# A new order table, loads cut differently and less in flight, in a fused attention and feed-forward kernel

## The chip, the cores and the metric

The kernel runs on one NeuronCore of a Trainium2 chip. The metric is the device time of one execution in microseconds (us). Three runs of the kernel before gave 119.25, 120.09 and 119.3 us, median 119.3. The profile is of one further execution, which took 120.38 us; its span on the core, from the first to the last instruction of the program, is 118.6 us, so 1.78 us lie outside the span.

## The reference

The inputs are q, k and v (4 batches, 4 heads, 1088 tokens, 32 features a head), two sketch matrices S1 and S2 (8 x 32), and two feed-forward weights w_in (128 x 2048) and w_out (2048 x 128), all float32.

```
phi(x) = outer(S1 x, S2 x)                 # 64 features per token
kv  = phi(k)^T v ;  z = sum over tokens of phi(k)
x   = phi(q) kv / (phi(q) . z + 1e-6)      # per batch and head, then 4352 x 128
h   = x @ w_in ;  out = (h - tanh(h)) @ w_out
```

So there are two parts: a linear attention whose softmax is replaced by squared sketches, and a feed-forward part with 16 hidden blocks of 128 for 4352 tokens. The term `h @ w_out` is taken as x @ (w_in @ w_out), computed once; that product is kept as a high and a low bfloat16 half (wch and wcl).

## The kernel before, in words

**Names of the work.** An operation has a name and a batch number b from 0 to 3. The k side of a batch is, in this order: kT (VectorE 32x32 transposes of the loaded k, L518), ksk (TensorE sketch, L538), kab (VectorE transposes of the sketch out of PSUM, L544), gram, gm, scmm, sc (a scale from the Gram matrix of the sketches, on TensorE and ScalarE, L559 to L571), three outer products w (VectorE or GpSimd, L579), three kvmm (TensorE, 12 float32 matmuls each, L594), and kvd, kvt, kvb (copies and a transpose of the sum). The q side is qT (VectorE transpose, L530), qsk (TensorE, L633), abc (VectorE transpose out of PSUM, L638), m, den, rd, ap (the division), qp (outer product, L676), qpT (VectorE transpose, L681), num (TensorE, L692), and x, the copies of the result from PSUM into the bfloat16 tile xT (L336). Batch 0 is cut into three pieces of 2, 3 and 4 blocks (num0.0, num0.2, num0.5), batch 1 into two (num1.0, num1.5); batches 2 and 3 are whole. All of this is float32.

**The feed-forward part** goes over ten groups of tokens, of 256, 384, 448, six times 512, and 192. The first three are exactly batch 0, so group 3 (the first of 512) needs the first piece of batch 1. For each group there are 16 matmuls h (L792), 16 tanh on ScalarE (th, L796; the last three groups take two blocks in one instruction), 18 accumulating matmuls o (16 with tanh, L807, and the two with wch and wcl, L811), one transpose ot (VectorE, L816), and stores (L826). The weights are cast to bfloat16 on ScalarE or GpSimd (L336, names wi0 to wi3 and wo0 to wo3); w_in is also transposed on TensorE (wit, L757) and copied (wiT), for the product w_in @ w_out (wc, L771).

**Order.** Nothing is decided while the kernel runs. A text table of some 830 tokens (TABLE) names each operation, the engine that does it, and the buffer that it takes. `plan` (L172) reads the table once; each engine does its share strictly in the table's order, and `sync` adds the semaphore waits. So an instruction that waits holds up all that is behind it on its engine, DMA issues on SyncE and ScalarE included. A token `f` stands for a filler: a matmul of a zero tile (zz, set by a VectorE memset, L398) into an unused bank (L399), which does no work and is there to keep TensorE busy.

**Loads.** All inputs are loaded once (8.8 MB). `load` (L426) adds a limit: before a load is issued, the one that lies CAP bytes of loads before it must have landed. CAP is 2.0 MB. All loads but the two of S1 and S2 are issued by SyncE.

```
load_k:  one DMA of 544 KB a batch (128 partitions)
load_v:  two DMAs a batch, 288 KB and 256 KB, 64 partitions each
load_q:  one of 544 KB a batch; batch 0 in two, 128 and 416 KB
load_wi, load_wo:  four of 256 KB each
```

Of the kernel before, what the change touches and what calls it, by code (L numbers as in the profile page):

```python
# [9 lines left out]
NC = 34  # L10
# [9 lines left out]
CAP = 2.0e6  # L20
# [5 lines left out]
42g 19s 18a 9g 15v 1g 20s 17a 44g 48g 21s 6g 46g 10g 8g 24s 7g 2g 23s 5v 27s 51v:0 52v 40v 28s 41v f f f f f f f f f f  # L26
f f f f f f f f f f f f f 54t:0 0v 13v 22s 16v 53v 26s 4v 50g 25s 56v:0 43g 55v 3g f f f f f 57t:0 62v:0 32s 58a:0
211a f f f 59t 31s 61v:1 60a f f f 70t:0 215a 219t:0 212a 81v f 220t 29s 71v:0 f f 86t:0 221a 63v:2 30s 72v:1 214a
87v:1 f f f f f f f 223t:0 213a 64t:0 73v:0 88v:0 65t 74v:0 89v:1 66t 75v:0 36s 90v:1 76v:0 67a:0 33s f f f f f 68t
91v:1 222t 77v:0 69a:0 f f 78t:0 224a 92v:1 34s 216g 104v:1 79a 80a f f f f f 237t:0 218g 93v:1 233t:1 235t:2 238a:0  # L30
47g 236a:1 f f f 231t:0 105v 217a 245t:2 94t:0 82s 232a:2 97v:2 246a:3 234a:4 255t:0 99v:0 239t:2 95a 247t:1 106t:0
96a 143v:0 248a:5 37s 256a:6 263t:0 38s 144v 240a:7 257t:1 241t:0 310t:2 35s 258a:8 145t:1 107v:1 242a:9 108v 311a:10
39s 225t:0 100v:0 113g:3 259t:1 226t 253t:2 98v 227t 264t 254a:11 265t 266t 146v:0 260a:12 251t:2 267t 286t:1 147v
228t 101t:0 115v:4 229a 287a:13 84s 153g:5 252a:14 230v 249t:1 14v 243t:0 177v:1 306t:2 103a 268t 250a:15 109t:2 85s
244a:16 148t:3 178v 288t:0 102a 83s 269t 149a:1 261t:1 110a:0 270t 307a:17 11g 114v:1 271t 272t 273t 262a:18 179t:0
289a:19 45g 12g 152v:0 274t 275t 357t:0 276t 316t:1 154g:2 277t 181v:1 298t:2 150t 180v 116t:1 299a:2 122v 117t 151a
358a:4 118t 317a:1 155t:0 49g 156t 119a:1 186v:3 157t 182t:3 111t 290t:0 187v:1 158a:0 300t:1 183a:1 120t 112a 159t
188v:4 189t:2 121a:1 160a:2 190t 301a:0 161v 191t 291a:7 184t 349t:1 192a:1 312t:0 278t 185a 193t 350a:9 195v 292t:2
279t 294t:1 194a:3 280t 123t:0 295a:16 281v:0 293a:3 371t:1 313a:5 341t:2 124v:0 318t:0 372a:15 319t 320t 296t:0
342a:14 353t:1 297a:11 365t:2 162t:0 125v:1 354a:6 366a:8 126v:0 302t:0 321t 314t:1 127v:0 303a:12 343t:2 322t 128v:0  # L40
304t:0 344a:18 323t 163v:1 305a:13 359t:2 324t 315a:19 325t 326t 308t:0 360a:7 345t:1 131v:1 327t 309a:3 361t:2 328t
129v:0 346a:16 367t:0 329t 330t 368a:11 331t 355t:1 132v:1 332t 362a:2 369t:0 333t 130v 356a:0 334t 335t 363t:2
370a:12 347t:1 133t:0 164v:0 364a:13 336v:1 348a:17 165v:1 373t:0 138v:2 374t 134a 351t:0 135a 375t 166v:1 376t 352a:3
139v:0 398t:1 400t:2 377t 399a:10 136v:1 378t 406t:0 401a:5 379t 167v:1 402t:1 380t 407a:19 137v 381t 382t 403a:1
424t:2 168v:0 416t:0 383t 425a:14 384t 385t 172v:2 412t:1 417a:18 408t:2 386t 414t:0 409a:16 170v:1 140t:0 413a:17
173v:1 415a:9 387t 396t:1 141a 388t 142a 171v 426t:0 397a:3 389t 390t 473t:2 427a:6 455t:1 391v:2 196t:0 474a:0 169v
395s 456a:4 461t:0 337s 453t:2 428t:0 197v:0 462a:7 339s 429t 418t:1 454a:2 392s 430t 420t:0 404t:2 394s 174t:0
421a:13 198v:1 340s 405a:8 199v:0 393s 419a:11 200v:0 338s 410t:0 201v:0 285s 463t:1 175a 176v 431t 432t 411a:12 433t
206v:2 422t:2 464a:15 434t 510t:0 435t 423a:3 204v:1 436t 457t:1 511a:10 437t 481t:2 202v:0 458a:5 451t:0 438t 482a:1
439t 512t:1 207v:0 440t 452a:8 514t:2 441t 513a:19 205v 442t 443t 515a:16 469t:0 475t:1 203v 444t 470a:12 445t 477t:2  # L50
476a:17 459t:0 446v:2 208t:0 478a:9 450s 460a:18 284s 506t:0 449s 210v 467t:1 508t:2 448s 507a:11 483t:0 209v 484t
468a:13 447s 471t:0 485t 509a:3 486t 465t:1 487t 472a:14 524t:2 488t 466a:6 621t:0 579t:0 525a:8 489t 526t:1 623t:1
580a:2 479t:2 620t 527a:4 490t 516t:0 480a:5 491t 624t 517a:18 492t 493t 532t:1 622a:3 494t 495t 496t 497t 625a:6
518t:0 498t 639t:0 499t 533a:15 500t 536t:2 519a:14 638t 501v:1 534t:1 627t:1 537a:0 522t:0 538t:0 535a:17 539t 520t:2
523a:9 567t:1 540t 521a:5 541t 542t 528t:0 568a:1 543t 544t 529a:11 575t:1 545t 640a:9 626t 546t 547t 530t:0 576a:3
548t 549t 577t:2 531a:10 550t 565t:1 578a:16 551t 552t 628a:4 630t:0 583t:0 553t 554t 584a:14 555t 573t:2 641t:1
566a:5 556v:2 571t:0 629t 574a:4 569t:1 559s 642t 503s 572a:11 597t:0 598t 564s 644t:1 570a:10 645t 581t:0 283s 631a:0
585t:1 505s 646t 599t 600t 502s 586a:15 675t:0 647t 643a:3 282s 601t 648t 504s 602t 603t 604t 582a:17 587t:1 674t
589t:0 588a:5 649t 605t 590a:10 606t 607t 676a:6 595t:1 591t:0 672t:1 608t 671t 592a:11 650t 651t 596a:4 633t:0 609t
673a:1 593t:0 610t 652t 611t 594a:16 632t 635t:1 612t 634a:4 613t 614t 636t 687t:2 615v:0 653t 637a:0 678t:0 654t 616s  # L60
677t 655t 686t 617s 679a:7 721t:1 722t 695t:0 656t 561s 657t 723a:5 658t 619s 681t:0 688a:8 680t 696t 683t:1 659t
682a:2 660t 684t 661t 690t:2 697t 685a:4 662v:1 698t 693t:0 699t 666s 689t 667s 700t 701t 691a:0 618s 702t 703t 724t:1
557s 704t 670s 725t 692t 669s 705t 719t:2 718t 694a:1 706t 664s 707t 560s 562s 708t 709t 720a:9 710t 563s 711t 726a:3
712t 558s 663s 727t:0 728t 734t:1 665s 730t:2 713v:0 731t 668s 742t:1 729a:6 733t 743t 732a:7 736t:0 714s 744t 745t
737t 735a:2 746t 747t 740t:2 739t 715s 748t 738a:4 749t 750t 751t 752t 753t 741a:8 754t 716s 755t 756t 757t 758t 759t
717s 760v:2 764a 761s 762a 763s
# [59 lines left out]
class _Op:  # L126
    __slots__ = ("engs", "fn", "deps", "users", "vals", "eng", "mode", "seq", "at", "known", "waits", "inc", "cnt",
                 "sem", "dma", "name", "lock")


class _Prog:
# [4 lines left out]
    def add(self, engs, fn, r=(), w=(), chain=None, dma=0, name="", after=(), mode=None, lock=False):  # L136
        o = _Op()
        o.engs = engs
        o.fn, o.dma, o.name, o.mode, o.lock = fn, dma, name, mode, lock
# [32 lines left out]
    def plan(self, table, filler):  # L172


        self.order = {e: [] for e in ENGINES.values()}
        at = 0
        seen = set()
        for token in table.split():
            at += 1
            if token == "f":  # L180
                o = _Op()
                o.engs, o.fn, o.mode, o.name, o.dma = {"tensor": 0}, filler[0], "128x128", "fill", 0
                o.deps, o.users, o.vals, o.lock = {filler[1]: True}, [], [], False
                e = "tensor"
            else:
# [4 lines left out]
                seen.add(o)  # L190
                picks = iter(picks.split(",")) if picks else iter(())
# [83 lines left out]
def _v(n):  # L275
    return {"vector": (n / 0.96 + 52.0, n / 0.96 + 195.0)}
# [14 lines left out]
def _as(n):  # L291
    return {"scalar": (n * 0.8333 + 70.0, n * 0.8333 + 214.0)}

# [13 lines left out]
def bass_polysketch_attn__then__act_tanh_shrink_kernel(  # L307
# [90 lines left out]
    zop = P.add(_v(192), lambda e, n: e.memset(zz.ap[:, :], 0.0), w=[zz], name="zz")  # L398
    filler = (lambda e, n: e.matmul(bank(3)[:, 0:256], zz.ap[:, 0:128], zz.ap[:, 128:384], start=True, stop=True), zop)  # L399
# [13 lines left out]
    for pl, f, val, nm in ((kT_p, lambda a: a[:, 1088:1152], 0.0, "kTz"), (m_p, lambda a: a[:, :, 8:9], 1e-6, "meps")):  # L413
        for i, s_ in enumerate(pl.choices):
            o = P.add(_g(40), lambda e, n, a=f(s_[1][0]), val=val: e.memset(a, val), name=f"{nm}{i}")
            pl.seed(i, o)
# [3 lines left out]
    vvals = [[_Val(ap=vL[b][e * 64:(e + 1) * 64, :, :]) for e in range(2)] for b in range(B)]  # L420
    for b in range(B):
        P.add(_v(128), lambda e, n, b=b: e.memset(vL[b][64:128, :, 256:288], 0.0), w=[vvals[b][1]], name=f"vpad{b}")

    loads = []

    def load(o_, i_, w, nbytes, rows, eng="sync", cap=True, name="", wait=()):  # L426
        after = list(wait)
        if cap:
            left = CAP - nbytes
            for op, nb in reversed(loads):  # L430
                left -= nb
                if left < 0:
                    after.append(op)
                    break
        op = P.add({eng: 80.0 + 2.1 * rows}, lambda e, n: e.dma_start(out=o_, in_=i_), w=w, dma=(nbytes, nbytes / rows),
                   after=after, name=name)
        if cap:
            loads.append((op, nbytes))
        return op

    for x, Sx in ((0, S1), (1, S2)):
        load(sin.ap[:, x, :], Sx[None, :, :].to_broadcast([16, 8, 32]), [sin], 16384, 128, "scalar", cap=False, name=f"sin{x}")
# [7 lines left out]
    def load_k(b):  # L450
        load(kL[b][:, :], k[b].rearrange("h (t c) d -> (h t) (c d)", c=NC), kvals[b], 128 * 1088 * 4, 128, name=f"lk{b}")
# [448 lines left out]
```

## Time and profile before

| what | value |
|---|---|
| median of three runs | 119.3 us |
| the profiled execution | 120.38 us, span 118.6 us |
| TensorE matmuls (PE) | 99.0 us busy, 84% of the span |
| ScalarE (ACT) | 82.6 us, 70% |
| VectorE (DVE) | 64.6 us, 54% |
| fillers (L399), part of PE's 99.0 | 59 matmuls, 10.4 us |
| loads and stores | 8.81 MB read, 2.23 MB written |
| mean granted clock of PE | 0.979 |

PE is the matmul unit, PEld its weight loads, which run beside the matmuls. A row of slices cuts the span into 40 equal parts of 2.97 us and gives each engine's busy share in tenths. PE's busy time counts matmuls whose ends are modelled, and fillers are in it, so a busy PE need not be doing useful work. A row of the chain names start, length and what the time went to; "issue" is time in which an engine waited for nothing that the profile shows.

### The profile page before, as it was taken

Reading aid. Unit: us, or ns where it says so; the run is one execution under the profiler, and the core shown is the slowest. Engines: PE = TensorE matmul, PEld = TensorE weight load, DVE = VectorE, ACT = ScalarE, POOL = GpSimd, SP = SyncE. Lnnn points to the kernel's source line nnn. Section 1 sums busy time; section 2 is a strip of 40 time slices with the busy share of each in tenths; the row PEclk is TensorE's granted clock in tenths of the full one; section 3 lists DMA queues with packets and bytes.
Section 4 is the critical chain, followed back from the end, with each engine's and each line's share of the span. In section 5 each row is a group of like instructions: output and inputs, shape, how many; then the busy total and the mean of one; then the engine's idle time right before and its main releaser. Section 6 shows DMA issues by size and latency. Waiting matters only on the chain.

```text
span 118.6 us, 3448 instructions
## 1 busy us (share of the span) xinstructions
PE 99.0 (84%) x1496; PEld 52.5 (44%) x1503; DVE 64.6 (54%) x106; ACT 82.6 (70%) x173; POOL 9.8 (8%) x28
## 2 busy tenths in 40 slices
PE   0069889749979858999999999999999999999920
PEld 0046458524545745334544444444444444445710
DVE  1360799995866993699999999630201000220210
ACT  3100383557337529899899899799999999997900
POOL 4020004001792000000000000000000000000000
PEclk9999999997699999999999999999999999999997
DMA  3799999999292000000000450140000350143555
GB/s 116 238 290 269 299 280 320 284 304 180 43 268 104 11 0 6 6 0 0 6 0 6 74 81 6 27 72 0 0 6 0 55 78 0 23 63 48 79 76 77
DMA packets 24637, 11.24 MB, mean 95 GB/s; under 512 B 18864, under 2 KB 23088, under 8 KB 24624
## 3 DMA queue, kind: packets, MB, share of 16 engines
q1 hardware_dynamic: 23920, 10.97, 38.2%
q8 instruction: 11, 0.18, 0.7%
q10 hardware_dynamic: 704, 0.08, 0.5%
q14 instruction: 2, 0.02, 0.0%
HBM read 8.81 MB, written 2.23 MB: 93 GB/s over the span
## 4 chain that ended last, share of the span: by engine, by line
PE 70%; DVE 15%; issue 5%; DMA 4%; ACT 1%
PE psb L807 23%; PE psb L792 23%; PE psb L692 7%; PE psb L399 5%; DMA kL<-in_k_dram 4%; DVE abc L638 3%; PE psb L594 3%; PE psb L811 3%; PE psb L538 3%; DVE w L579 2%; DVE qpT L681 2%; DVE qp L676 2%; PE psb L633 1%; PE psb L771 1%; DVE m L650 1%
## 5 line engine op out<-in xcount | busy, mean ns | idle before, releaser
L796 ACT ACTIVATE th<-psb 128x512 bf16<-128x512 f32 (+4 forms) x136 | 70.2, 623 | 7.3 <-PE psb L792 5.9
L792 PE MATMUL psb<-xT,wi 128*128 128x512 bf16 (+4 forms) x154 | 44.9, 352 | 0.6 <-issue 0.3
L807 PE MATMUL psb<-th,wo 128*128 128x512 bf16 (+4 forms) x159 | 42.9, 348 | 0.2
L816 DVE STREAM_TRANSPOSE ot<-psb 128x512 f32<-128x512 f32 (+4 forms) x10 | 6.3, 629 | 33.6 <-PE psb L807 33.6
L792 PEld LDWEIGHTS psb<-xT,wi 128*128 128x128 bf16 x160 | 14.9, 98 | 21.1 <-ACT th L796 10.9
L807 PEld LDWEIGHTS psb<-th,wo 128*128 128x128 bf16 x160 | 15.2, 98 | 13.1 <-issue 1.4
L399 PE MATMUL psb<-zz 128*128 128x256 bf16 x59 | 10.4, 323 | 7.0 <-DVE zz L398 7.0
L692 PE MATMUL psb<-qpT,kvb 32*32 32x128 f32 (+4 forms) x448 | 8.8, 309 | 3.4 <-issue 2.5
L681 DVE STREAM_TRANSPOSE qpT<-qp 128x768 f32<-128x768 f32 (+1 forms) x14 | 11.3, 832 | 0.0
L676 DVE TENSOR_TENSOR qp<-ap,abc 128x768 f32<-128x768 f32 (+1 forms) x14 | 11.0, 818 | 0.0
L399 PEld LDWEIGHTS psb<-zz 128*128 128x128 bf16 x59 | 6.1, 115 | 9.5 <-DVE zz L398 7.0
L579 DVE TENSOR_TENSOR w<-abk 128x768 f32<-128x768 f32 x9 | 8.1, 936 | 0.0
L692 PEld LDWEIGHTS psb<-qpT,kvb 32*32 32x32 f32 x448 | 5.2, 103 | 6.3 <-issue 3.0
L569 ACT COPY gm<-psb 128x32 f32<-128x32 f32 x4 | 0.7, 189 | 10.5 <-PE psb L559 10.5
L544 DVE STREAM_TRANSPOSE abk<-psb 128x288 f32<-128x288 f32 x8 | 3.4, 462 | 7.0 <-PE psb L538 7.0
L518 DVE STREAM_TRANSPOSE kT<-kL 128x576 f32<-128x576 f32 (+1 forms) x8 | 5.5, 721 | 2.9 <-DMA kL<-in_k_dram 2.9
L336 ACT CAST xT<-psb 128x192 bf16<-128x192 f32 (+4 forms) x11 | 3.7, 376 | 4.5 <-PE psb L692 4.5
L594 PE MATMUL psb<-w,vL 128*32 128x64 f32 x288 | 5.0, 220 | 1.8 <-issue 1.8
L638 DVE STREAM_TRANSPOSE abc<-psb 128x1152 f32<-128x1152 f32 (+2 forms) x5 | 5.6, 1125 | 1.1 <-PE psb L633 1.1
L579 POOL TENSOR_TENSOR w<-abk 128x768 f32<-128x768 f32 x3 | 5.2, 1722 | 10.7 <-DVE abk L544 10.7
L594 PEld LDWEIGHTS psb<-w,vL 128*32 128x32 f32 x288 | 4.4, 110 | 2.2 <-issue 2.1
L530 DVE STREAM_TRANSPOSE qT<-qL 128x1088 f32<-128x1088 f32 (+2 forms) x5 | 5.2, 1065 | 0.0
(52 smaller groups left out, 59.1 us busy)
## 6 DMA issues: line engine op xcount, KB each, us to landing
kL<-in_k_dram SPq DMA_DIRECT2D x4, 544.0 KB, 4.7
qL<-in_q_dram SPq DMA_DIRECT2D x3, 544.0 KB, 6.1
vL<-in_v_dram SPq DMA_DIRECT2D x4, 288.0 KB, 5.8
wi_f<-in_moe_w_in_dram SPq DMA_DIRECT2D x4, 256.0 KB, 5.6
wo_f<-in_moe_w_out_dram SPq DMA_DIRECT2D x4, 256.0 KB, 5.9
vL<-in_v_dram SPq DMA_DIRECT2D x4, 256.0 KB, 6.6
out_dram<-ot SPq DMA_DIRECT2D x16, 64.0 KB, 2.0
out_dram<-ot SPq DMA_DIRECT2D x8, 56.0 KB, 1.9
```

Source lines behind the costliest of these rows:

```text
L399: filler = (lambda e, n: e.matmul(bank(3)[:, 0:256], zz.ap[:, 0:128], zz.ap[:, 128:384], start=True, stop=True), zop)
L518: P.add(_v(nb * 64), lambda e, n, e_=e_, nb=nb: e.transpose(kT[b].ap.rearrange("p (j u t r) -> p r j u t", u=2, t=32, r=2)[:, :, 0:nb, e_, :],
L579: P.add({**_v(768), **_g(768, 2.2)} if WPOOL[b] else _v(768), lambda e, n: e.tensor_tensor(out=wv.ap.rearrange("p (x i j) -> p x i j", i=8 ...
L594: i = e.matmul(pv[b].ap[h * 32:(h + 1) * 32, 0:64], vL[b][:, h, blk * 32:(blk + 1) * 32], wvs[b, p].ap[:, (bi * 4 + h) * 64:(bi * 4 + h + ...
L638: P.add(_vp(sn * 4), lambda e, n: e.transpose(abc.ap.rearrange("p k h f -> p h k f")[:, :, 0:s1 - s0, :], psa4[:, :, 0:sn].rearrange("p h ...
L676: P.add(_v(cn * 256), lambda e, n, qp=qp, c0=c0, cn=cn: e.tensor_tensor(out=qp.ap[:, 0:cn * 256].rearrange("p (x i j) -> p x i j", i=8, j= ...
L681: P.add(_v(cn * 256), lambda e, n, qp=qp, o0=o0, cn=cn: e.transpose(qt.ap[:, o0 * 256:(o0 + cn) * 256], qp.ap[:, 0:cn * 256]), r=[qp], w=[ ...
L692: i = e.matmul(psa4[h * 32:(h + 1) * 32, g, 0:nb * 32], kvb.ap[g * 32:(g + 1) * 32, x, h * 32:(h + 1) * 32], qq[g * 32:(g + 1) * 32, 0:nb, ...
L792: P.add(_mm(n_), lambda e, n, jb=jb, hv=hv: e.matmul(hv.ap[:, jb % m * 512:jb % m * 512 + n_], wi[jb // 4].ap[:, (jb % 4) * 128:(jb % 4 + ...
L796: P.add(_a(n_ * m), lambda e, n, hv=hv, th=th: e.activation(out=th.ap.rearrange("p (u x) -> p u x", u=m)[:, :, 0:n_], in_=hv.ap.rearrange( ...
L807: fn = lambda e, n, x=x, st=st, sp_=sp_: e.matmul(ov.ap[:, 0:n_], wo[x // 4].ap[:, x % 4, :], ths[x][0].ap[:, ths[x][1] * 512:ths[x][1] * ...
L816: P.add(_vp(n_), lambda e, n: e.transpose(ot.ap[:, 0:n_], ov.ap[:, 0:n_]), r=[ov], w=[ot], name=f"ot{gi}")
```

## The change

Five things change together.

1. CAP goes from 2.0 to 1.4 MB, and the limit is now applied in table order over both issuing engines.
2. The load of k for batch 0 is cut in two halves of 272 KB (lk0.0, lk0.1), and its VectorE transposes into four, two a half. The load of S2 (sin1) moves from ScalarE's queue to SyncE's, behind these two halves.
3. v comes in four loads of 144 KB a batch, one a head, of 128 partitions with 288 columns each; the two halves of the partitions overlap by 32 columns, which replaces the zero padding of v (four memsets go; zeros in kT move to another place). Loads of v, of q and of w_in may be issued by ScalarE or SyncE.
4. A second filler, `F`, has 512 columns. The tile zz is written first of all.
5. The order table is new throughout. By its own account it was made with a model of instruction fetches.

The order that the new table gives, where the prediction needs it:

```
SyncE    lk0.0 lk0.1 sin1 lq0.0 lv0.1 lwi2 lwo0 lwo1 lq0.1 lv1.0 lwo2 lwo3 lk1 lk2 lv2.0 lk3 [st0.0] lv2.1 lv2.2 lq2.0 ...
ScalarE  sin0 lv0.0 lwi0 lwi1 lv0.2(waits lk0.0) lv0.3(waits lk0.1) lwi3(waits lwi0) [table load] wi0 wi1 gm0 sc0 wi2 wi3
         wo0 kvd0 wo1 kvb0 wiT0 x0.0 x0.0 wiT1 | tanh group 0 | lv1.1(waits lk2) wch x0.2 x0.2 lq1.0(waits lv2.0) th lv1.2(waits lk3)
         lv1.3 ... lv3.0(waits lv1.2) gm2 lv3.1 lv3.2(waits lv2.1) ... lv3.3(waits lv2.2) ... tanh group 2, x1.0
TensorE  f F*10 ksk0 wit0 gram0 f F scmm0 F qsk0.0 kvmm0 (wit1, wit2 between) F F kvt0 F F F num0.0 wit3 qsk0.2 h0.0 ...
         ... qsk1 | groups 2's h and o, all but two | num1.0 o2 o2 h3.0 ...
VectorE  zz mask4 kT mask2 kT kT kT stt wab qT0.0 kab0 kab0 w w abc0.0 m w den rd ap qp qpT qT0.1 abc0.2 m den rd ap qp ...
```

In the table before, zz stood behind wab on VectorE; the chain of the second piece (abc0.2, m, den, rd, ap) and qT0.1 stood between the steps of the first; and h matmuls of later groups were mixed among earlier ones. The diff, without the table:

```diff
-CAP = 2.0e6
+CAP = 1.4e6
...
+        loads = []
...
-            if token == "f":
+            if token in "fF":
...
+                if o.big:
+                    left = CAP - o.dma[0]
+                    for p in reversed(loads):
+                        left -= p.dma[0]
+                        if left < 0:
+                            o.deps.setdefault(p, False)
+                            break
+                    loads.append(o)
...
-    zop = P.add(_v(192), lambda e, n: e.memset(zz.ap[:, :], 0.0), w=[zz], name="zz")
+    zop = P.add({"vector": (1.0, 1.0)}, lambda e, n: e.memset(zz.ap[:, :], 0.0), w=[zz], name="zz")
...
+               "F": lambda e, n: e.matmul(bank(3), zz.ap[:, 0:128], zz.ap[:, None, 128:384].to_broadcast([128, 2, 256]),
...
-    for b in range(B):
-        P.add(_v(128), lambda e, n, b=b: e.memset(vL[b][64:128, :, 256:288], 0.0), w=[vvals[b][1]], name=f"vpad{b}")
...
-        load(kL[b][:, :], k[b].rearrange("h (t c) d -> (h t) (c d)", c=NC), kvals[b], 128 * 1088 * 4, 128, name=f"lk{b}")
+            for r in range(2):
+                load(kL[b][:, r * 544:(r + 1) * 544], src[:, r * 544:(r + 1) * 544], [kvals[b][r]], 128 * 544 * 4, 128, name=f"lk{b}.{r}")
...
-        for e in range(2):
-            w_ = 256 if e else 288
-            load(vL[b][e * 64:(e + 1) * 64, :, 0:w_], vs[:, :, e * 288:e * 288 + w_], [vvals[b][e]], 64 * w_ * 16, 256, name=f"lv{b}.{e}")
+        for h in range(H):
+            src = bass.AP(tensor=vs.tensor, offset=vs[:, h, :].offset, ap=[[256, 2], list(vs.ap[0]), [1, 288]])
+            load(vL[b][:, h, :], src, [vvals[b][h]], 128 * 1152, 128, DQ, name=f"lv{b}.{h}")
...
+            for r0, r1 in (((0, 1), (1, 2)) if b == 0 else ((0, 2),)):
```

## The prediction

> **What bounds the kernel now.** I read the slices first, for where engines stand still, then the chain for what they wait on, then the busy time by windows. Slices, and the row of instruction fetches from the queue table:
>
> ```profile
> PE   0069889749979858999999999999999999999920
> ...
> DVE  1360799995866993699999999630201000220210
> ACT  3100383557337529899899899799999999997900
> ...
> PEclk9999999997699999999999999999999999999997
> ...
> q8 instruction: 11, 0.18, 0.7%
> ```
>
> From slice 16 (47 us) on PE is full; the losses lie before, and in the first 7 us PE does nothing. The chain, in order of time (start, length, what):
>
> ```profile
> 0.73 4.26 DMA kL<-in_k_dram
> ...
> 6.74 0.22 DVE zz L398
> 7.00 4.73 PE psb L399 x23
> 11.73 0.73 PE psb L538 x16
> ...
> 24.75 1.67 issue
> ...
> 33.58 0.87 issue
> ...
> 41.21 1.77 issue
> ```
>
> Three things are to be seen. (a) The zero tile is written at 6.74, so the 23 fillers in front of the first sketch ksk0 run from 7.00 to 11.73, though its operand wab was there at 6.74: ksk0 (11.66 by the timeline) is some 4.9 us late for work that does nothing. (b) In three places PE has an open instruction stream and no instruction, 4.3 us in all. Counted in the trace, the first two lie 256 instructions (weight loads and matmuls together) apart, and the third 512 further on; 0.18 MB in 11 packets is 16 KB a packet. I read them as late instruction pages. (c) The rest is in the timeline and the windows (busy time and count of PE, PEld, DVE, ACT, POOL; granted clock; DMA):
>
> ```profile
> 23.40 0.66 ACT L796 ACTIVATE th<-psb 128x256 bf16<-128x256 f32 x2 [0.38 <-PE psb L792]
> ...
> 57.27 0.76 ACT L336 CAST xT<-psb 128x320 bf16<-128x320 f32 x2 [0.39 <-PE psb L692]
> ```
>
> ```profile
> 17.39:56.06 38.67, 32.77 (x808) 19.71 (x805) 31.80 (x52) 24.62 (x71) 7.80 (x10) 0.96 0.44 119
> 23.40:57.27 33.87, 28.82 (x706) 16.32 (x705) 27.00 (x42) 22.55 (x66) 6.33 (x7) 0.95 0.33 84
> 57.27:113.40 56.13, 55.38 (x474) 26.02 (x480) 23.11 (x34) 52.80 (x94) 0.00 (x0) 1.00 0.22 33
> ```
>
> The first tanh starts at 23.40. Groups 3 to 9 need batch 1, whose first piece reaches xT from 57.27. Between 17.39 (abc0.2) and 56.06 (num1.0), DVE is busy 31.80 of 38.67 us: the q and k sides of the batches go through DVE, so DVE bounds this stretch, with 6.9 us idle. From 57.27 to the last matmul at 113.4 PE is busy 55.4 of 56.1 us and ACT 52.8. The last 5.2 us are ot and the stores. So the time is: first x1.0, plus 56.1, plus 5.2.
>
> **Part 1, the head.** In the changed order zz is DVE's first instruction; before, DVE's first (a memset) starts at 0.82. With 0.22 for zz the fillers start at about 1.1 instead of 7.00. Eleven fillers of 256 + 10 x 512 columns are 21 x 256; at 4.73/23 = 0.206 us per 256 that is 4.3 us, over at 5.5. Nothing waits for them, since wab is later. k0 in halves: the bytes are the same, so I let the second half land where all of k0 did, 4.99; the first half's transposes hide under that. Behind it come half of 0.72 and one of 0.65 = 1.0 us instead of 1.37, then stt 0.20 and wab 0.19 with small gaps: wab at 6.45 (before 6.74). S2, third on SP's queue, is issued at 0.73 + 2 x 0.40 = 1.5; with the 4.5 us of the sin row it lands at 6.0, as stt is due; bounds 0 and +0.6 (two such issues), I take 0. So ksk0 starts at 6.6, against 11.66: **5.1 us earlier**.
>
> From ksk0 to abc0.0. Before, kab ended 1.68 us after ksk0's start, so gram0 could run at 8.3. But wit0 now stands ahead of it on PE and needs wi0, which ACT casts behind seven DMA issues, the last of which waits for lwi0, and behind the table load. lwi0 is issued at about 1.9 (two issues at 0.61 to 0.64) and takes the 5.6 us of its row: 7.5; plus an issue 0.5, the table load 1.28, the cast 0.62: 9.9; wit0 0.40: gram0 at 10.3, 2.0 us held. From gram0 to qsk0.0 it was 1.35 us (13.39 to 14.74): 11.65, and with 0.39 and a hand-over of 0.15 abc0.0 starts at 12.2 (before 16.07). Then DVE does abc 0.41, m 0.21, w 0.92, den 0.19, rd 0.19, ap 0.21, qp 0.62, qpT 0.70 = 3.45, with eight hand-overs of 0.06: 16.1 (before 21.56, as qT0.1 and the second piece's chain stood between). num0.0 0.84: 17.0. kvb0 must be there too: kvmm0.2 follows w0.2 (13.9), and kvd, kvt, kvb took 2.2 us from kvmm's end (19.5) to num (21.7): 14.4 + 2.2 = 16.6 at the worst, no matter. Two xT copies 0.43 and wiT1, 1.02, stand ahead of the first tanh: **18.5 instead of 23.40**. On DVE qT0.1 (1.04) follows qpT, 17.15; qsk0.2 (0.67) then, and abc0.2 starts at 18.1 (before 17.39). So DVE starts its long stretch later than before, which is why the 5 us don't simply arrive.
>
> **Part 2, to x1.0.** The changed order has 45 DVE instructions from abc0.2 to the last qpT before num1.0. Each has its row here; without the 0.08 by which neighbours overlap they come to 30.2 us. So num1.0 is at 18.1 + 30.2 = 48.3 plus DVE's idle time. Before, that was 6.9. Its causes are PE results that come late (ksk, kvmm, qsk), and late pages are 4.3 of them. Bounds: 0 if every result is in time, 6.9 if the new order does no better. I take 4.7, half of the late pages gone: num1.0 at 53.0 and x1.0 at 54.2 (1.2 later, as before): **3.1 us earlier**. A page can't be fetched faster by an order; from a fetch's start to the next instruction it was 2.4 to 2.75 us, and fetches began 1 to 5.6 us after the page before was entered.
>
> [...]
>
> **Part 3, after x1.0.** Groups 3 to 9 have the same forms. Before, 18 matmuls o of group 2 were still to come at num1.0, at 0.19 each 3.4 us; now two. That takes 3.0 us of PE off: 53.1. ACT needs 52.8 for the same tanh. Both full at once can't be had, so between 53.1 and 56.1 I take 54.5: **1.6 us less**. The tail stays 5.2.
>
> **Part 4, loads.** v costs 4 x 144 = 576 KB a batch for 544, 0.13 MB more in all, under 0.5 us at the 290 GB/s of slice 2 and hidden under the head's other loads; without that cover it is those 0.5. CAP 1.4 MB: at 290 GB/s it is 4.8 us of transfer, and loads took 4.7 to 6.6 us from issue to landing, so it is about at the edge. Gain or loss lies between -0.5 and +2 us (1.4/6 us = 233 GB/s for the 3.3 MB to lq0.1, 2.5 us later, of which 0.5 are slack); nearest are the 4.7 of k, so I take 0. The eight DMA issues that now stand among ACT's tanh cost it 0.40 to 0.64 each, 4 us. ACT has 22.55 us of work between first tanh and x1.0, so 26.6 of now 35.7: hidden, 9.1 us left. The four memsets (0.17 each, one of which, vpad0, opened DVE's order) cost nothing before or after. GpSimd has two outer products instead of three, DVE one more (0.92, in the 30.2).
>
> **Sum.** x1.0 54.2 + 54.5 + 5.2 = 113.9, against the span of 118.6: -4.7 us, 115.7 for the profiled execution. The median shown is 1.1 below the profiled run, so on it I forecast 119.3 - 4.7 = **114.6**. Bounds: DVE idle 0 to 6.9 gives -4.7 and +2.2, part 3 -1.4 and +1.6, the loads -0.5 and +2.
>
> **Rivals.**
> 1. *DVE hardly waits.* For it: the order was spread so that holes fall elsewhere. Idle 1.5 (-3.2) and part 3 at 53.8 (-0.7): 110.7. Chance 0.12.
> 2. *The clock falls back.* For it: after the first hole the granted clock falls in slices 9 and 10, at 7 and 6 tenths; now PE stands idle from 5.5 to 6.6 and, for wi0, from 7.3 to 9.9. PE work on the path from 9.9 (wit 0.40, scmm 0.25, qsk0.0 0.39, num0.0 0.84, qsk0.2 0.67) at half rate costs up to 2.5, I take 2.3: 116.9. Chance 0.11. [...]
> 3. *A page is late in num0.0.* Counting on from the holes, a page ends after two thirds of num0.0, and the one before is entered in kvmm0.0 at about 11.9. With the slower latency seen (4.8 + 2.5) it comes at 19.2, not 16.2: 3.0 us on PE, on qsk0.2 and so on DVE: 117.6. Chance 0.12.
> 4. *The table does not do what it says:* a second hole, in num0.2, of 1.9 as there before: 119.5, no change. Chance 0.08.
> 5. *Slower: ACT stands in waits for loads.* Six of its DMA issues among the tanh wait for a landing. SP's such waits took 17.1 us in 7, the longest 5.4. ACT has 9.1 us to spare, and the kernel is slower by 1% from 9.1 + 4.7 + 1.2 = 15.0 us of waits. Three of 5.4 make 16.2, so 7.1 late: 121.7. Against it: these loads are issued long before ACT comes there. Chance 0.12.
>
> ```profile
> SPq L435 <- DMA qL<-in_q_dram: 7.7, 2, 5.4
> ```
>
> **Numbers.** The forecast has 0.45. Faster by over 1% (under 118.1; 1% is about what a measurement of this kernel can tell from no change): 0.45 + 0.12 + 0.11 + 0.12 = 0.80; within 1% 0.08; slower 0.12. The forecast's own range is 112.5 to 116.8; to hold 8 in 10 it goes from 111.3 to 118.8, which leaves out the best case's best, most of case 4, and case 5.
>
> **What would show it.** ksk0 at 6.6 and fillers from 1.1 (part 1 wrong if ksk0 is after 8); first tanh at 18.5; abc0.2 at 18.1; x1.0 at 54.2 with DVE idle 4.7 before; x1.0 to the last matmul 54.5; ACT's waits for loads near 0. I am wrong if a hole stands in num0.0, if wi0 is cast after 12, or if x1.0 stays at 57.

## The result, and the profile after

The changed kernel took 142.9 us (median of four, 141.78 to 144.57); the kernel before, beside it, 119.69 (119.25 to 121.43). The ratio is 1.192, 95% interval 1.18 to 1.204: **slower by 19%**, where I had forecast 114.6 us. The profiled execution has a span of 142.6 us and a mean granted clock of 0.856 (before 118.6 and 0.979). It took 144.57 us, the longest of the four, and the run that is set against it below was profiled in the shortest of its four, so their spans lie 33.2 us apart where the medians lie 30.1 apart.

Slices (each 3.57 us; I count them from 0) and rows of the changed kernel's page. The `GB/s` row is what the DMA engines moved, the `DMA` row the mean busy share of the 16 engines in tenths:

```profile
PE   6620538999893049200799998999999999999991
...
PEclk9985555799999655955559999999999999999999
DMA  4615741984621441111101530220404004040415
GB/s 143 214 49 177 190 139 57 254 233 173 172 68 48 117 138 56 48 48 49 48 0 18 94 104 5 37 32 11 63 5 74 0 7 71 0 74 5 66 22 85
...
L604 PE MATMUL psb<-w,vL 128*32 128x64 f32 x288 | 9.3, 309 | 21.6 <-DMA vL<-in_v_dram 21.6
...
vL<-in_v_dram ACTq DMA_DIRECT2D x10, 144.0 KB
...
vL<-in_v_dram SPq DMA_DIRECT2D x6, 144.0 KB
wi_f<-in_moe_w_in_dram ACTq DMA_DIRECT2D x3, 256.0 KB, 9.0
```

The same rows of the kernel before:

```profile
DMA  3799999999292000000000450140000350143555
GB/s 116 238 290 269 299 280 320 284 304 180 43 268 104 11 0 6 6 0 0 6 0 6 74 81 6 27 72 0 0 6 0 55 78 0 23 63 48 79 76 77
...
L594 PE MATMUL psb<-w,vL 128*32 128x64 f32 x288 | 5.0, 220 | 1.8 <-issue 1.8
...
vL<-in_v_dram SPq DMA_DIRECT2D x4, 288.0 KB, 5.8
...
vL<-in_v_dram SPq DMA_DIRECT2D x4, 256.0 KB, 6.6
```

TensorE stands still in four places, and the wait that was not there before is that of the kvmm (L604, before L594): 21.6 us of idle time that ended with a landing of v, where before it was 1.8 us without a landing. In slices 16 to 19, from 57.0 to 71.3 us, the DMA engines move 48 or 49 GB/s while their mean busy share is one tenth. Before, slices 2 to 8 moved 269 to 320 GB/s at a share of nine tenths. So I read the low rate as that of some two busy engines of 16, and not as a limit of the memory.

The chain of the changed kernel (start, length, what), its windows (busy time and count of PE, PEld, DVE, ACT, POOL; clock; DMA share; GB/s) and TensorE's waits (in total, times, longest):

```profile
4.32 17.66 DMA vL<-in_v_dram
...
52.24 16.14 DMA vL<-in_v_dram
```

```profile
28.35:85.86 57.51, 37.44 (x757) 20.60 (x757) 31.93 (x48) 24.69 (x68) 4.24 (x4) 0.79 0.30 89
...
58.10:68.50 10.40, 0.02 (x4) 0.06 (x5) 1.31 (x1) 1.62 (x5) 0.00 (x0) 0.63 0.14 48
85.86:139.27 53.41, 52.95 (x463) 24.25 (x463) 24.73 (x36) 50.81 (x91) 0.00 (x0) 1.00 0.21 32
```

```profile
PE psb L604 <- DMA vL<-in_v_dram: 21.6, 3, 10.7
PE psb L767 <- ACT wi L349: 8.0, 1, 8.0
```

Two single v loads stand on the chain for 17.66 and 16.14 us; before, a v load landed 5.8 to 6.6 us (medians of its two sizes) behind its issue. From 58.1 to 68.5 TensorE did 0.02 us of work, the DMA share was 0.14 (2.2 of 16 engines) and the rate 48 GB/s. A batch of v is 4 x 147,456 B, so at 48 GB/s it takes 12.3 us.

The semaphores point the same way. (A semaphore is the counter that tells a waiting engine that data is there.) Counted in the trace, the semaphore of a load is raised in 16 separate steps in the kernel before. In the changed kernel each of the 16 v loads has only three: one at once, and two when the data is there (lv0.3: 8.61, then 20.26 and 21.98 us). And a v load does not only delay itself. The first load of w_in, whose semaphore has 16 steps, has 14 of them between 5.45 and 6.77 us and the last two at 9.15 and 10.81. With v spread out (first experiment) all 16 came between 5.59 and 7.12. The trace fits two engines that are shared and full, so that every load waits for its slowest share. ScalarE's next issue of w_in, which stands ahead of wi0's cast, waited for this landing until 10.83 us and then took 3.09 us itself (7.14 and 0.33 in the first experiment). So wi0's cast came at 15.25 us, not at the 9.3 that I had worked out, and that is the 8.0 us wait above.

Why two: the source of a v load in the diff is `[[256, 2], list(vs.ap[0]), [1, 288]]`, whose outermost count is 2, and its semaphore shows one step, then two. In the runs below, with 4, 8 and 64 in that place, it shows 1 + 4, 1 + 8 and 16 steps. The prediction had not weighed that count.

To see where the 23 us went, I cut every run at three marks: x0.0 (the first cast to xT), x1.0 (the first cast of batch 1), and the start of the last matmul.

| profiled run | x0.0 at | x0.0 to x1.0 | x1.0 to last matmul | behind it | span |
|---|---|---|---|---|---|
| before | 22.59 | 34.68 | 55.80 | 5.5 | 118.6 |
| changed | 28.35 | 57.51 | 53.41 | 3.3 | 142.6 |
| changed, v on 16 engines | 17.47 | 35.18 | 53.41 | 3.3 | 109.4 |

Up to x1.0, where v is needed, the changed kernel is slower than before, and behind it faster.

### The profile page after: what moved, and what is told of

Same layout as the page of the kernel before. It is cut to its first block, busy times and chain, and to the rows that moved or that the text cites. A ratio compares the mean times of both kernels' runs of the same rounds, so it can differ in the third digit from the quotient of the medians.

```text
span 142.6 us, 3390 instructions
## 1 busy us (share of the span) xinstructions
PE 105.3 (74%) x1463; PEld 52.2 (37%) x1463; DVE 67.3 (47%) x107; ACT 82.1 (58%) x171; POOL 7.5 (5%) x27
## 4 chain that ended last, share of the span: by engine, by line
PE 52%; DMA 26%; SPq 9%; DVE 8%; ACT 3%; issue 1%
DMA vL<-in_v_dram 24%; PE psb L817 18%; PE psb L802 17%; SPq L440 6%; PE psb L604 5%; PE psb L702 4%; SPq L836 3%; PE psb L821 2%; DMA kL<-in_k_dram 2%; PE psb L643 2%; ACT th L806 2%; DVE kT L528 2%; DVE qp L686 1%; DVE qpT L691 1%; PE psb L413 1%; DVE ot L826 1%
## 5 line engine op out<-in xcount | busy, mean ns | idle before, releaser
L802 PE MATMUL psb<-xT,wi 128*128 128x512 bf16 (+4 forms) x160 | 48.3, 354 | 0.9 <-ACT th L806 0.4
L817 PE MATMUL psb<-th,wo 128*128 128x512 bf16 (+4 forms) x160 | 46.2, 357 | 0.1
L604 PE MATMUL psb<-w,vL 128*32 128x64 f32 x288 | 9.3, 309 | 21.6 <-DMA vL<-in_v_dram 21.6
L604 PEld LDWEIGHTS psb<-w,vL 128*32 128x32 f32 x288 | 7.7, 169 | 22.5 <-issue 19.1
L589 DVE TENSOR_TENSOR w<-abk 128x768 f32<-128x768 f32 x10 | 9.6, 988 | 5.4 <-PE psb L604 5.3
L767 PE MATMUL psb<-identb,wi 128*128 128x128 bf16 x16 | 2.2, 285 | 8.0 <-ACT wi L349 8.0
L413 PE MATMUL psb<-zz 128*128 128x512 bf16 x17 | 7.6, 586 | 0.0
L581 ACT COPY wq<-psb 128x8 f32<-128x8 f32 x4 | 0.7, 166 | 10.1 <-PE psb L575 10.1
L528 DVE STREAM_TRANSPOSE kT<-kL 128x576 f32<-128x576 f32 (+3 forms) x10 | 5.5, 598 | 1.9 <-DMA kL<-in_k_dram 1.9
L349 ACT CAST wi<-wi_f 128x512 bf16<-128x512 f32 x4 | 2.4, 618 | 5.0 <-DMA wi_f<-in_moe_w_in_dram 5.0
## 6 DMA issues: line engine op xcount, KB each, us to landing
qL<-in_q_dram SPq DMA_DIRECT2D x2, 544.0 KB, 10.7
```

What stands on the lines that cost most here:

```text
L413: "F": lambda e, n: e.matmul(bank(3), zz.ap[:, 0:128], zz.ap[:, None, 128:384].to_broadcast([128, 2, 256]), start=True, stop=True)}, zop)
L528: P.add(_v(nb * 32 * (r1 - r0)), lambda e, n, e_=e_, nb=nb, r0=r0, r1=r1: e.transpose(kT[b].ap.rearrange("p (j u t r) -> p r j u t", u=2, ...
L589: P.add({**_v(768), **_gt(768)} if WPOOL[b] else _v(768), lambda e, n: e.tensor_tensor(out=wv.ap.rearrange("p (x i j) -> p x i j", i=8, j= ...
L604: i = e.matmul(pv[b].ap[h * 32:(h + 1) * 32, 0:64], vL[b][:, h, blk * 32:(blk + 1) * 32], wvs[b, p].ap[:, (bi * 4 + h) * 64:(bi * 4 + h + ...
L802: P.add(_mm(n_), lambda e, n, jb=jb, hv=hv: e.matmul(hv.ap[:, jb % m * 512:jb % m * 512 + n_], wi[jb // 4].ap[:, (jb % 4) * 128:(jb % 4 + ...
L817: fn = lambda e, n, x=x, st=st, sp_=sp_: e.matmul(ov.ap[:, 0:n_], wo[x // 4].ap[:, x % 4, :], ths[x][0].ap[:, ths[x][1] * 512:ths[x][1] * ...
```

## Experiments

**1. v on 16 engines.** The same table, limit, bytes and packets (128 of 1152 B a load). Only the shape of a v load changes: half the partitions of two heads, instead of all partitions of one.

```diff
-            src = bass.AP(tensor=vs.tensor, offset=vs[:, h, :].offset, ap=[[256, 2], list(vs.ap[0]), [1, 288]])
-            load(vL[b][:, h, :], src, [vvals[b][h]], 128 * 1152, 128, DQ, name=f"lv{b}.{h}")
+            e, g = h % 2, h // 2 * 2
+            load(vL[b][e * 64:(e + 1) * 64, g:g + 2, :], vs[:, g:g + 2, e * 256:e * 256 + 288],
+                 [vvals[b][h]], 128 * 1152, 128, DQ, name=f"lv{b}.{h}")
```

> The changed kernel with one thing undone: each of v's four loads a batch is a pair of heads by one half of the partitions (64 partitions x 2 x 288 columns) in place of one head by both halves (2 x 64 x 288). Bytes (144 KB), packets (1152 B), queues, order table and CAP are as in the changed kernel. Theory E (a v load of the changed kernel runs on 2 of the 16 DMA engines, since its outermost count is 2: its semaphore gets 3 updates where other loads get 16): each v semaphore gets 16 updates, the holes of 10.7 and 6.8 us ahead of kvmm go, and the time falls from 142.9 to what the blind prediction worked out without them, 111 to 119 us. Theory O (ScalarE standing in waits for loads, and the smaller CAP, are the cause, whatever the loads' shape): the time stays above 135.

Measured: 112.76 us (111.36 to 113.15), the kernel before 119.02; ratio 0.9435, interval 0.9285 to 0.9585. From its page:

```profile
GB/s 95 277 291 273 252 257 260 288 139 206 176 140 300 194 8 0 50 219 12 6 0 89 1 0 92 4 6 96 0 0 11 85 6 50 46 0 53 43 61 74
...
vL<-in_v_dram ACTq DMA_DIRECT2D x10, 144.0 KB, 4.2
...
vL<-in_v_dram SPq DMA_DIRECT2D x6, 144.0 KB, 4.6
```

252 to 291 GB/s are back in slices 1 to 7, at a DMA share of eight or nine tenths, a v load lands 4.2 to 4.6 us behind its issue (medians), and its semaphore has 16 steps. The one edit is worth 30 us of 142.9. The rest of the change is a gain of 5.7% (by the interval, 4.2 to 7.2).

**2 and 3. The same pattern in the kernel before, and a control.** Here v's loads are read with an outermost count of 2, and in the control as 64 rows of the same length. Both move 6% more bytes of v than the kernel before, and v holds other rows than it should in both, so that part of the output is not the reference's. The four memsets of v's padding write to a spare tile in both.

```diff
-            w_ = 256 if e else 288
-            load(vL[b][e * 64:(e + 1) * 64, :, 0:w_], vs[:, :, e * 288:e * 288 + w_], ...
+            src = bass.AP(tensor=vs.tensor, offset=vs[:, :, e * 288:].offset, ap=[[256, 2], [544, 32], [1, 1152]])
+            load(vL[b][e * 64:(e + 1) * 64, :, :].rearrange("p h x -> p (h x)"), src, ...
# control: ap=[[544, 64], [1, 1152]]
```

> The kernel before, with its two v loads a batch read as 2 x 32 rows of 1152 floats (outermost count 2) in place of 64 rows x 4 x 288 or 256. The order, the queue and CAP are as before; v holds other rows than the reference wants, and 6% more of them. Theory E: 2.36 MB through two engines at the 24 KB/us each that the changed kernel shows (48 GB/s in its quiet slices) are 49 us, and with these engines' share of the other loads (0.4 MB each, 17 us) the last v lands near 66 instead of 37, so kvmm3 is some 22 us later than its 44: 130 to 145 us. Theory O: as before, 119 to 121.

> Control of the run with outermost count 2: the same bytes and the same packets of 4608 B, but read as 64 rows of 1152 floats, outermost count 64; v again holds other rows than the reference wants. Both theories: 119 to 121 us, as the kernel before. If it is slow too, the packets or the rows are to blame and not the count.

Measured: 151.36 us (ratio 1.276, 1.259 to 1.294), and the control 119.84 (1.0105, 0.994 to 1.027). The page of the run with count 2:

```profile
DMA  5714882868111151111000000060130005113446
GB/s 172 228 49 144 190 201 77 262 217 254 63 45 54 55 161 59 52 57 53 35 4 0 0 4 0 15 103 14 27 52 0 4 0 79 26 16 52 68 62 92
```

Again some 50 GB/s at one tenth over most of slices 10 to 19, without the new table, the new limit or v on ScalarE's queue. Its last v landed at 73.12 us, not near 66, and the time lies 6 us above the 130 to 145 that I had expected: the direction was right, the sum too small. No other part of the change is needed for the loss.

**4 and 5. The dose.** The changed kernel with 4 x 32 and 8 x 16 rows in place of 2 x 64; destination, packets, queues and table stay as they are. v holds other rows in both.

```diff
-            src = bass.AP(tensor=vs.tensor, offset=vs[:, h, :].offset, ap=[[256, 2], list(vs.ap[0]), [1, 288]])
+            src = bass.AP(tensor=vs.tensor, offset=vs[:, h, :].offset, ap=[[256, 4], [544, 32], [1, 288]])
# and ap=[[256, 8], [544, 16], [1, 288]]
```

> The changed kernel with the source of each v load written as 4 x 32 rows instead of 2 x 64 (outermost count 4); the same 128 packets of 1152 B, the same destination, queues, order and table; v holds other rows than it should, so this part of the output is not the reference's. THEORY (number of DMA engines): the transfer runs on 4 engines, its semaphore gets a jump and 4 updates. In the changed kernel a v packet took 52.6 ns, so the 16 v loads keep each of their engines busy 16 x 32 x 52.6 ns = 26.9 us instead of 53.9; the other loads add 21.0 us per engine until the last v (run with 16 engines): 48 us, against 39 when the last v landed there. So the last v lands at about 48 (71.7 in the changed kernel) and the end comes 5 to 10 us after that of the 16-engine run: 117 to 123 us. RIVAL (the interleaved source or the 1152 B packets themselves are slow, whatever the count): as the changed kernel, 139 to 145 us. RIVAL (only k = 2 hurts, for a reason of its own): as with 16 engines, 111 to 114 us.

> The changed kernel with the source of each v load written as 8 x 16 rows (outermost count 8); the same 128 packets of 1152 B, all else the same; v holds other rows than it should, so this part of the output is not the reference's. THEORY (number of DMA engines): 8 engines, a jump and 8 updates; the v loads keep each busy 13.5 us, with the 21.0 us of the other loads 34.5, under the 39 us at which the last v landed with 16 engines: nothing is late by this sum, 112 to 115 us. RIVAL (the pattern itself is slow): 139 to 145 us.

Measured: 123.9 us (122.52 and 125.28; too few for an interval; 117 to 123 was expected) and 112.83 (ratio 0.9425, 0.925 to 0.960; 112 to 115 expected). The page of the run with 4:

```profile
DMA  3758489862557222000540040050220050501425
GB/s 100 217 183 252 151 239 283 244 222 49 191 150 201 100 90 97 33 0 16 73 161 5 0 67 13 0 85 0 48 43 0 9 81 0 85 0 21 64 42 78
```

In the slices from 40 to 49 us there are two tenths and 90 to 100 GB/s: twice the share and twice the rate. Over two engines there and four here that is some 24 GB/s an engine, an estimate from the 48 and the 90 to 100.

| outermost count | steps of a v semaphore | last v landed | time |
|---|---|---|---|
| 2 | 1 + 2 | 71.7 | 142.9 |
| 4 | 1 + 4 | 51.2 | 123.9 |
| 8 | 1 + 8 | 41.6 | 112.8 |
| 64 (run 1) | 16 | 39.0 | 112.8 |

The packets are as in the changed kernel at 4 and 8, and the rows overlap in the same way, so neither is the cause; the count is, and shares and rates fit two engines at 2 and four at 4. At 8 the loads are hidden again: the work per engine, if there are eight, by my estimate 13.5 us of v (16 loads x 16 packets x 52.6 ns, the mean of a v packet in the changed kernel) and 21.0 of the other loads and stores (run 1, until its last v), stays under 39. At 4 that sum was 48, and the last v landed at 51.

**6 and 7. The first four loads, and the other twelve.** From run 1's kernel, with the pattern of count 2 in batch 0 alone (`if b == 0`), or in all the others (`if b > 0`).

```diff
+            if b == 0:
+                src = bass.AP(tensor=vs.tensor, offset=vs[:, h, :].offset, ap=[[256, 2], list(vs.ap[0]), [1, 288]])
+                load(vL[b][:, h, :], src, [vvals[b][h]], 128 * 1152, 128, DQ, name=f"lv{b}.{h}")
+            else:
```

> The changed kernel with only the four v loads of batch 0 in its own form (outermost count 2) and the other twelve on 16 engines. THEORY 1 (what counts is when the last v lands: in the four runs so far the last matmul started 66 to 69 us behind it): the two engines have 4 x 3.37 + 5.0 + 21.0 = 39.5 us of work against 39 us, so they catch up, the last v lands at 39 to 42, and the end is 112 to 116 us. THEORY 2 (the late start itself: the first tanh was at 29.8 us in the changed kernel and 18.9 with 16 engines, and this is never made good): 8 to 11 us more than with 16 engines, 120 to 124 us.

> The changed kernel with the four v loads of batch 0 on 16 engines and the other twelve in its own form (outermost count 2). THEORY 1 (the last v sets the end): the two engines have 12 x 3.37 + 4 x 0.42 + 21.0 = 63 us of work, the last v lands at about 63, the last matmul starts 67 us behind it, and with the 6 us behind and around that the time is 133 to 138 us, although the first tanh is back near 19. THEORY 2 (the late start counts for 11 us of the 30): the 20 that are left, 130 to 134 us. If only the first part counted: 112 to 114.

Measured: 123.15 us (ratio 1.043, 1.033 to 1.053) and 134.55 (1.1395, 1.132 to 1.147). The windows of the run with the first four, and then of the run with the other twelve:

```profile
27.04:63.99 36.95, 34.17 (x757) 18.05 (x757) 31.61 (x48) 24.68 (x68) 4.04 (x4) 0.95 0.47 132
63.99:117.41 53.42, 52.97 (x464) 24.27 (x463) 24.73 (x36) 50.81 (x91) 0.00 (x0) 1.00 0.21 32
```

```profile
18.44:75.62 57.18, 36.12 (x757) 19.84 (x757) 32.07 (x48) 24.66 (x68) 5.11 (x6) 0.85 0.30 89
75.62:129.04 53.42, 52.97 (x463) 24.23 (x463) 24.74 (x36) 50.81 (x91) 0.00 (x0) 1.00 0.21 32
```

The first four cost 9.6 us up to x0.0 (27.04 for 17.47) and 1.8 behind it; the other twelve cost 1.0 up to x0.0 and 22.0 between x0.0 and x1.0. Together 34 us between profiled executions, and the changed kernel had 33.2 more span than run 1. So the loss is two losses that add up: late wi0 and late v of batch 0 in front of the first piece, and late v of batches 1 to 3 before x1.0.

My first theory for the pair of runs fell with the first of them. In the four runs of the dose table the last matmul started 66 to 69 us behind the last v, so I took the last v for what sets the end, and expected 112 to 116 us with the first four. The second run can't tell the two theories apart: its 134.55 us lies in the 133 to 138 of the first and 0.6 above the 130 to 134 of the second, and its last v landed at 62.57. With the first four, too, the last matmul started 68.7 us behind the last v (117.41 less 48.76), but for another reason: the last v came late because it was *issued* late, its issue starting at 44.8 us and not at 35.4, on ScalarE's queue, which was itself late. TensorE's idle time in this run:

```profile
PE psb L772 <- ACT wi L349: 5.5, 1, 5.5
PE psb L609 <- DVE qp L691: 3.4, 1, 3.4
PE psb L553 <- DVE wab L505: 3.2, 1, 3.2
PE psb L609 <- issue: 1.7, 1, 1.7
```

The 3.4 us are the first kvmm: the profile names qp, which ended at 21.01, but the last v of batch 0 landed at 21.14 and the matmuls started at 21.2. Behind the head there is one wait at a kvmm, 1.7 us, which ended as a late-issued v landed. VectorE needs 31.6 of the 37 us that follow, so there is little room to make good what the head loses.

**8. The limit back at 2.0 MB**, in run 1's kernel.

```diff
-CAP = 1.4e6
+CAP = 2.0e6
```

> The changed kernel with v on 16 engines (as in the run of that edit: 112.8 us) and the loads' limit put back from 1.4 to 2.0 MB in flight. THEORY (with v on 16 engines the limit hardly counts; only the table and the fillers gave the gain): within 1.5 us of that run, 111.5 to 114.5 us. RIVAL (the limit is what brings the first w_in chunk, landed 7.12, and the last v, 38.95, in time: more in flight shares the engines between more loads): wi0's load lands 1 to 2 us later, 114.5 to 116 us.

Measured: 112.92 us (112.1 to 113.68), ratio 0.944 (0.928 to 0.960). The limit makes no difference that can be measured.

**9. Only the early zero tile, in the kernel before.** The token of zz moves to the head of the old table.

```diff
-42g 19s 18a 9g 15v ...
+0v 42g 19s 18a 9g 15v ...
```

> The kernel before with one token of its table moved: zz is VectorE's first instruction. By part 1 of the prediction the 23 fillers then run from 1.1 to about 5.9, ksk0 starts at 6.8 instead of 11.66. If the head were bound by that alone, 4.9 us would arrive: 114.5. Loads that were covered by the fillers show up next (wi3, wi2 and wo land at 14 to 18.5 and don't move), so I expect 115.5 to 118. A rival, that the stretch after the head doesn't start earlier for the loads, gives 119 to 120.

Measured: 116.75 us (113.85 to 117.12; no interval can be given). The wab tile was ready at 6.27 and ksk0 started at 6.32, not 11.66; x0.0 came at 19.02 instead of 22.59, x1.0 at 53.28 instead of 57.27, and the last stretch was 55.80 as before. So the early fillers alone are worth 4.0 us of span between the profiled executions, and 2.3 us between the medians (119.02 for the kernel before), inside the 115.5 to 118 us expected; the gain is not known better than that.

**10 to 12. Rival 2, the clock.** In run 1 TensorE was idle between ksk0 and the transposes of wi0, and the granted clock was 0.5 from 9.60 to 13.02. Five more wide fillers were put there:

```diff
-... 49g 48g 50g 226t:0 51g ...
+... 49g 48g 50g F F F F F 226t:0 51g ...
```

> The changed kernel with v on 16 engines and five more wide filler matmuls on TensorE between the last ksk0 matmul and the first transpose of w_in's chunk 0, where TensorE stood idle 6.82 to 9.46 us and after which the granted clock was 0.5 from 9.60 to 13.02. THEORY (rival 2 of the prediction: the idle stretch brings the clock down and this costs): the clock stays at 1.0 until after 13; TensorE's 72 kvmm0, 32 first qsk0 and 16 transposes in that stretch run up to twice as fast, abc0.0 (12.76) starts 0.5 to 1.5 us earlier and the end follows: 111 to 112.5 us. RIVAL (the clock's fall there is hidden, since kvmm0 and qsk0 wait for VectorE and ScalarE): 112 to 113.5 us, no change. RIVAL (the fillers don't keep the clock, or they delay wi0's transposes): 113 to 114 us.

Measured: 112.23 us (110.54 to 113.57). The window from 9.0 to 13.5 of this run, and of run 1:

```profile
9.00:13.50 4.50, 4.25 (x146) 2.84 (x147) 4.14 (x10) 2.69 (x7) 0.00 (x0) 1.00 0.90 265
```

```profile
9.00:13.50 4.50, 3.94 (x93) 2.29 (x93) 2.74 (x6) 2.84 (x7) 0.00 (x0) 0.62 0.93 261
```

The clock stays at 1.0 (run 1: 0.62), TensorE gets through 146 matmuls instead of 93 and VectorE is busy 4.14 us instead of 2.74. x0.0 came at 15.94 instead of 17.47, x1.0 at 51.81 instead of 52.65. The time itself lies in the ranges of both theories (111 to 112.5 and 112 to 113.5). To see how much of it is more than chance, both kernels ran once more side by side:

> The changed kernel with v on 16 engines once more (112.76 us before), beside the one with five more fillers, to compare the two on one chip. Without a change of state: 111.5 to 113.5 us.

> The same with the five fillers more (112.23 us before; granted clock 1.0 throughout, abc0.0 at 11.23 instead of 12.76, x0.0 at 15.94 instead of 17.47, but the first tanh at 18.14 instead of 18.89 and x1.0 at about 51.8 instead of 52.65). THEORY (the clock's fall costs, and 0.8 us of it reach the end): 0.4 to 1.2 us under the run beside it. RIVAL (nothing reaches the end): within 0.4 us of it.

Measured: 112.74 us (111.88 to 114.59; ratio 0.951, 0.944 to 0.958) without, 112.14 (110.54 to 115.7; 0.945, 0.935 to 0.955) with the fillers. The intervals overlap, so a gain of 0.6 us is neither shown nor excluded. In this second profile of the fillers the page gives the clock as 1.0 throughout, but that is no measurement for the head: the trace has no record of the clock there before 13.51 us (in the first profile, before 4.66), and the matmuls before it ran slowly. ksk0 took 1.21 us and the five fillers 2.31, where in the first profile they took 0.72 and 1.25, and from 9.0 to 13.5 us TensorE got through 38 matmuls, not 146. In the kernel before, 16 matmuls of ksk's form took 0.72 us at a granted clock of 1.0 (from 27.57) and 1.21 at 0.5 (from 29.27). So I take the clock to have been at 0.5 in the head of this execution, in spite of the fillers; w_in's first load landed at 8.60 instead of 6.62 as well, and x0.0 came at 19.09. So what the five fillers did for the clock seems to have differed between the two executions. In the five profiles of the new table with v on 16 engines (runs 1, 8 and 10 to 12), x0.0 lies between 15.94 and 19.09 us and the span between 108.6 and 110.6, and the later x0.0 goes with the longer span (the two latest have the same). That fits some two thirds of a delay in the head reaching the end; no run tests it.

## Why the prediction was wrong

**The step that failed is part 4**, and in it one sentence: "v costs 4 x 144 = 576 KB a batch for 544, 0.13 MB more in all, under 0.5 us". I priced the new loads by their bytes, at the rate of loads that had another pattern, and called them hidden. The kernel before has no load with an outermost count under 16 (16, 64 and 128 in its code, and each of its loads raised its semaphore in 16 steps), so its 290 GB/s was no price for this one; the prediction should have called the new pattern unseen and bounded it. What the runs showed in its place: v came at 48 GB/s and a DMA share of 0.14, TensorE waited 21.6 us for it at the kvmm and 8.0 us for wi0, and the term that I put at 0 was 30.1 us between the medians (142.9 against 112.76) and 33.2 us of span (142.6 against 109.4). The range that I gave the loads was -0.5 to +2.

**Rival 5** had the right kind of cause, loads that land late, and in the main the wrong place. I asked who waits on ScalarE's queue among the tanh. ScalarE did wait, in the head: the issue of w_in that waits for the first one, and took 3.09 us, put the table load at 13.95 us and wi0's cast at 15.25 (8.80 in run 1), past the 12 that I had named as a sign of being wrong. But more was decided by TensorE's own wait for the data, 21.6 us, and no term of mine had it.

The other steps can be read in run 1, where nothing but the pattern of v differs (and in the changed kernel, in brackets, where they are not covered up).

| step | predicted | run 1 (changed) |
|---|---|---|
| ksk0 starts | 6.6 | 6.50 (7.29) |
| w_in's first load landed | 7.5 | 7.12 (10.81) |
| gram0 | 10.3 | 10.07 |
| abc0.0 | 12.2 | 12.76 (19.21) |
| qpT0.0 ends | 16.1 | 16.44 |
| num0.0 | about 16.2 | 16.59 (27.46) |
| first tanh | 18.5 | 18.89 (29.76) |
| abc0.2 | 18.1 | 18.81 |
| x1.0 | 54.2 | 52.65 (85.86) |
| x1.0 to the end of the last matmul | 54.5 | 53.7 (53.7) |
| behind it | 5.2 | 3.1 (3.1) |

**Part 1** held to 0.4 us in the first tanh. The row of ksk0, and the windows of run 1:

```profile
6.50 0.72 PE L549 MATMUL psb<-kT,wab 64*32 64x288 f32 x16 [0.72 <-DVE wab L501]
```

```profile
17.47:52.65 35.18, 32.76 (x757) 17.41 (x757) 31.72 (x48) 24.68 (x68) 4.66 (x6) 1.00 0.51 147
18.81:51.44 32.63, 30.40 (x656) 16.09 (x654) 30.51 (x46) 22.70 (x65) 3.76 (x3) 1.00 0.52 147
52.65:106.06 53.41, 52.96 (x463) 24.27 (x463) 24.73 (x36) 50.80 (x91) 0.00 (x0) 1.00 0.20 32
```

**Part 2**: from abc0.2 to num1.0 VectorE is busy 30.51 us, against my 30.2, and idle 2.1, against my 4.7. That is close to rival 1 (1.5). **Rival 3** did not happen: num0.0 ran from 16.59 to 17.4 without a hole. TensorE had one wait of the "issue" kind over 1 us, of 1.2, where before there had been 1.67, 0.87 and 1.77. It ended at 37.88 us, 2.6 us behind the start of an instruction fetch and 0.1 us behind the landing of a v load, so the trace does not tell whether it was a late page. A second hole (rival 4) did not come in this profile either.

**Part 3** ended 0.8 lower, with the same 53.4 us to the start of the last matmul in all ten profiles of the new table, and TensorE busy for 52.96 of it in run 1. I had taken a middle between 53.1 and 56.1. **The tail** I had left at 5.2, and it was 3.1. The stores of the last groups fit it, in a row of the timeline of the kernel before and one of the changed:

```profile
112.70 4.10 SPq L826 DMA_DIRECT2D out_dram<-ot  x8
```

```profile
138.57 2.20 SPq L836 DMA_DIRECT2D out_dram<-ot  x4
```

Before, eight issues on SyncE's queue stood in a row there, and the last one started 2.6 us behind the end of the last ot; the new order leaves four, and the last two start within 0.4 us of it.

**Rival 2** did happen in run 1: the clock was 0.5 for 3.4 us after the idle stretch, the half rate of the rival's sum, as in the kernel before from 28.30 to 31.71 us. Its price, 2.3 us, is not settled: with the clock up, x0.0 came 1.5 us earlier and the span was 0.8 us shorter; between the two executions with fillers, of which the second had the clock late and w_in's load late, the span differs by 2.0; and the medians with and without fillers differ by 0.6, which is not clear of chance. The fall at slice 9 of the kernel before had no such idle stretch ahead of it: there TensorE was busy for 1.88 of the last 3.41 us (24.89 to 28.30), where in run 1 it was busy for some 0.7 (ksk0). The limit in **part 4** (CAP) cost nothing that could be measured, as taken.

So without v's pattern the forecast of 114.6 would have been 1.8 us too high (112.8 measured), inside the range. In the span of run 1's profile, its shortest execution, the misses come to 4.5 us (113.9 forecast, 109.4): x1.0 1.5, part 3 0.8 and the tail 2.1 us earlier, all to one side.

## What to carry to other kernels

Price a new load by its access pattern, not by its bytes alone: look at the outermost count of its source, and where the profile has no load of that kind, bound it by one engine's rate (here some 24 GB/s, an estimate: half of the 48 measured with a count of 2) as well as by the rate of the rows seen. In these profiles the sign was 48 GB/s at a DMA share of 0.14 while TensorE waited for a load; the steps of the semaphore without the first, 2 with a count of 2 and 4 with 4, went with a share of 2.2 engines of 16 and of two tenths. When a version with a good idea is slower, undo its parts one by one: here one line of the change took 30 us and hid a gain of 5.7% in the rest.

## What the runs showed of the hardware

- A load whose source had an outermost count of 2, 4 or 8 raised its semaphore in 1 + 2, 1 + 4 and 1 + 8 steps; alone, such loads moved 48 GB/s at a DMA share of 0.14 with 2, and 90 to 100 at two tenths with 4.
- The loads with a count of 2 also slowed one whose semaphore has 16 steps: 14 of the steps of w_in's first load came by 6.77 us, the last two at 9.15 and 10.81 (all by 7.12 in run 1).
- The granted clock fell to 0.5 within or just behind waits of TensorE, also late in the program: in run 1 from 9.60 to 13.02 us, behind a wait of 2.3 that ended at 9.56, and in the changed kernel from 9.54 to 26.61, 47.09 to 57.33 and 60.74 to 74.40 us, around waits of 8.0, 7.9 and 10.7 us. In the changed kernel it stayed down each time for 5 to 11 us behind the wait. Waits for loads so cost a second time, in the matmuls behind them (a weight load of kvmm took 177 ns in the median, its shortest 110).
- In the 3.41 us ahead of the three falls in the changed kernel TensorE was busy for 0.72, 0.41 and 0.45 us, and ahead of the one in the kernel before for 1.88. All the stretches between two changes of the clock in the changed kernel last 3.41 us or a whole multiple of it.
- From one execution to the next, the first load of w_in landed at 6.62 to 8.60 us in four executions of two programs that differ by five fillers, and x0.0 at 15.94 to 19.09, so a gain of half a microsecond in the head cannot be told from chance by one profile of each.
